# Two transformer layers with memory attention on one core: first segment in two token halves, loads tied to attention units, one pool of tiles, queries and keys projected two segments ahead

## The chip, the cores and the metric

The kernel runs on one core of a Trainium2 chip. A core has a matrix engine (TensorE, PE in the profile), a vector engine (VectorE, DVE), a scalar engine (ScalarE, ACT), a general engine (GpSimd, POOL) and an engine that issues transfers (SyncE, SP); ACT and POOL issue transfers too. Each engine has its own list of instructions, written in a fixed order, and waits on semaphores where the program says so. The matrix engine writes to PSUM, which the kernel takes as one tensor of 128 x 4096 f32, cut into eight banks of 512 columns; everything else is kept in SBUF. The metric is device time in microseconds.

## The reference

Two layers, each an attention block A and a feed-forward block B with the same weights, over 2048 tokens of width 512. Attention has 32 heads of width 16 and goes over the tokens in four segments of 512: causal attention inside a segment, and a memory of all earlier segments.

```python
q, k, v = heads(x @ wq), heads(x @ wk), heads(x @ wv)      # [B, H, N=4, L=512, 16]
phi = lambda t: jnp.where(t > 0, t + 1.0, jnp.exp(t))
g = sigmoid(beta)
for s in range(N):
    logits = einsum('bhqd,bhkd->bhqk', qs, ks) * scale + mask
    a_dot = einsum('bhqk,bhkd->bhqd', softmax(logits), vs)
    num = einsum('bhld,bhde->bhle', phi(qs), M)
    den = einsum('bhld,bhd->bhl', phi(qs), z)[..., None] + 1e-06
    outs.append(g * num / den + (1.0 - g) * a_dot)
    M = M + einsum('bhld,bhle->bhde', phi(ks), vs)
    z = z + einsum('bhld->bhd', phi(ks))
A = concat(outs) @ wo
B = (silu(x @ w1) * (x @ w3)) @ w2                          # width 1376 between
# x = x + A(layernorm(x)); x = x + B(layernorm(x)); both once more
```

## The kernel before

**A planner writes the order.** build() does not emit instructions. It adds operations to a list, each with the engines that may run it, an estimated duration, what it reads and writes, the tiles (bufs) that it holds, and a priority (lower goes first). schedule() then plays the list through once before anything is emitted: it lets each engine take, among the operations whose inputs would be there soon, the one of lowest priority, and so fixes one list for each engine. Tiles come from pools (ring()): an operation that needs a new tile is taken when one is free. finalize() derives the semaphore waits from the true dependences alone. Two things only steer the planner: a gate says that an operation may not be planned before another one has been, and a hold reserves a tile early. A gate leaves no wait in the program: on the chip, an operation with a gate starts as soon as its engine comes to it.

**The work of one segment.** A global segment g = 4 * layer + s has these stages:

- layer_norm (xa): statistics (bn_stats, bn_aggr) on VectorE, a power on POOL, the normalised tile xn on VectorE, and for each of four tiles of 128 tokens a transposing transfer xa<-xn issued by SP.
- project: twelve jobs of four matmuls each with 512 columns, in the order q0 k0 q1 k1 v0 v1 v2 v3 q2 k2 q3 k3 (the number is a group of eight heads for q and k, a token tile for v). Each job fills one PSUM bank of pool B (four banks); ACT or VectorE, whichever the planner picks, evicts it. km is a copy of k in which the even heads are zero: for g of 0 and 1 by VectorE, later by four transfers.
- phi: features of q and k: exp on ACT (px), two operations on VectorE (pq, pk).
- memory_read, for s > 0: 16 small matmuls give the denominators, VectorE takes reciprocals (rm), then four groups of matmuls give numerators, each in its own bank of pool B, each taken off by one VectorE operation (om).
- attention: 20 units. Each unit is a group of matmuls for logits (R in the planner, 16 and 32 rows of the array each) into pool S, one exp on ACT over 128 x 2048 elements, masks on POOL where a block touches the diagonal; every few units a group of matmuls with v (C) follows, an eviction xs, a transposing transfer xg<-xs, a normalisation og and a transposing transfer ot<-og. The list HALVES holds segment 0: it is done in two token halves, six units and fourteen, and, through SPLIT, with two exps of 1024 for each unit.
- memory_update: transposes of pk (pkt<-pk), matmuls with v, an addition to macc, a masked copy mb.
- out_proj: 16 matmuls with wo, added to x_tok on VectorE.
- layer_norm (xf) and ffn: 88 matmuls for gate and up, tanh on ACT, two VectorE operations each, and 44 matmuls down, added to x_tok. The priorities of ffn are the weakest; its matmuls fill PE while attention waits for ACT, and what is left is done at the end.

**What decides when projections come.** In project, job n of segment g is gated to attention unit (3n)//2 of segment g - 1 (line 547 and after). The layer_norm of g is gated to unit 10 of g - 2.

**Tiles of 4 KB per partition.** They lie in separate rings: xa 2, xf 1, q 2, k 2, pq 1, pk 1, pkt 1, ot 1, and km 2.

**Loads.** At the start SP issues x0, x2, wq, wv; ACT issues x1, x3, wk, x4 to x7, beta. late_loads gives the rest to POOL: wo, x8 to x11, x12 to x15, w1, w3 and w2 in halves and a remainder. Its gates name attention units of segment 0, so the planner puts the loads between POOL's masks, but no wait follows from them. wo comes out first on POOL.

**Constants.** clear_slot zeroes a va tile and writes ones for the denominators: slot 0 on VectorE, slot 1 on POOL by later_constants, which also clears km slot 1 and macc on POOL.

Of the kernel before, what the change touches and what calls it, by code (L numbers as in the profile page):

```python
# [59 lines left out]
class Sched:  # L60
# [15 lines left out]
    def add(self, opts, fn, reads=(), writes=(), bufs=(), prio=0.0, mode=None, dmaq=None, name="", gates=(), size=0,  # L76
            hold=()):
# [17 lines left out]
        for w in writes:  # L95
            p = self.res_w.get(w)
            if p is not None:
                deps[p.seq] = p
            for rd in self.res_r.get(w, ()):
                if rd is not op:  # L100
                    deps[rd.seq] = rd
            self.res_w[w] = op
            self.res_r[w] = []
        op.deps = deps
# [246 lines left out]
def build(nc, A_x, A_wq, A_wk, A_wv, A_wo, A_beta, B_w1, B_w3, B_w2, out):  # L351
# [26 lines left out]
    xa_r = ring("xa", 2, [P, NCG, 512])  # L378
    xf_r = ring("xf", 1, [P, NCG, 512])
    q_r = ring("q", 2, [P, NCG, 512])  # L380
    k_r = ring("k", 2, [P, NCG, 512])
    km_r = ring("km", 2, [P, NCG, 512])
    pq_r = ring("pq", 1, [P, NCG, 512])
    pk_r = ring("pk", 1, [P, NCG, 512])
    px_r = ring("px", 2, [P, 2, 512])
    pkt_r = ring("pkt", 1, [P, NCG, LT, P])
# [6 lines left out]
    ot_r = ring("ot", 1, [P, NCG, 512])  # L393
# [66 lines left out]
    def clear_slot(i, eng, gates):  # L460
        z = eng(lambda e: e.memset(va_r[i][:], 0.0), 3104, writes=[("va0", i)], prio=-50.0, gates=gates)
        o = eng(lambda e: e.memset(vheads(va_r[i], slice(0, LT), 0, H)[:, :, :, 16:17], 1.0), 128, writes=[("va0", i)], prio=-50.0,
                gates=gates)
        pools["va"].prev[i] = [z, o]

    clear_slot(0, dve, [])

    def later_constants(gates):
        clear_slot(1, pool, gates)
        pools["km"].prev[1] = [pool(lambda e: e.memset(km_r[1][:], 0.0), 2048, writes=[("km0", 1)], prio=0.5, gates=gates)]  # L470
        pool(lambda e: e.memset(macc[:], 0.0), 544, writes=[("macc", 0), ("macc", 1)], prio=1.0, gates=gates)
# [3 lines left out]
    for i in range(4):  # L475
        dma(("sp", "act")[i % 2], x_tok[:, i, :], xv[:, i, :], 131072, prio=CP - 10 + i, writes=[("x", i)], name="ldx%d" % i)

    def ldw(q, t, src, key, prio, gates=(), reads=()):
        dma(q, t[:], src.rearrange("(g p) f -> p g f", p=P), 524288, prio=prio, writes=[key], reads=reads, name="ld" + key)
    ldw("sp", wq_sb, A_wq, "wq", CP + 1)  # L480
    ldw("act", wk_sb, A_wk, "wk", CP + 2)
    ldw("sp", wv_sb, A_wv, "wv", CP + 3)
# [3 lines left out]
    def late_loads(after):  # L486
        for i in range(2, 4):
            dma("pool", x_tok[:, 4 * i:4 * i + 4, :], xv[:, 4 * i:4 * i + 4, :], 524288, prio=CP + i, gates=[units[(0, 8 * i - 9)]],
                writes=[("x", 4 * i + j) for j in range(4)], name="ldx")
        ldw("pool", wo_sb, A_wo, "wo", CP + 1.5, gates=[units[(0, 3)]])  # L490
        for a in range(2):
            for n, (t, src, key) in enumerate(((w1_sb, B_w1, "w1"), (w3_sb, B_w3, "w3"))):
                dma("pool", t[:, 2 * a:2 * a + 2, :], src[256 * a:256 * a + 256, :].rearrange("(g p) f -> p g f", p=P), 704512,
                    prio=CP + 4, gates=[units[(0, 5 + 4 * a + 2 * n)]], writes=[key + str(a)], name="ld" + key)
        for a in range(2):
            dma("pool", w2_sb[:, 5 * a:5 * a + 5, :], B_w2[640 * a:640 * a + 640, :].rearrange("(t p) d -> p t d", p=P), 655360,
                prio=CP + 6, gates=[units[(0, 13 + 2 * a)]], writes=["w2%d" % a], name="ldw2")
        dma("pool", w2_sb[0:96, 10, :], B_w2[1280:1376, :], 98304, prio=CP + 7, gates=[units[(0, 17)]], writes=["w22"], name="ldw2")
# [9 lines left out]
    def layer_norm(s, name, prio, gates=(), fine=False, part=(0, LT), dst=None):  # L508
        st = new("ln")
        dst = dst or new(name)  # L510
        tiles = range(*part)
        dt_ = {"xa": xa_r, "xf": xf_r}[name]
# [23 lines left out]

    class Seg:
        pass

    def project(s, g, X, first):  # L540
        z = Seg()
        z.q, z.k, z.km, z.va = new("q"), new("k"), new("km"), new("va")
        jobs = [("q", 0), ("k", 0), ("q", 1), ("k", 1), ("v", 0), ("v", 1), ("v", 2), ("v", 3),
                ("q", 2), ("k", 2), ("q", 3), ("k", 3)]
        if first:
            jobs = [("q", 0), ("k", 0), ("q", 1), ("k", 1), ("v", 0), ("v", 1), ("q", 2), ("k", 2), ("q", 3), ("k", 3),
                    ("v", 2), ("v", 3)]
        for n, (kind, G) in enumerate(jobs):
            p0 = g - 0.95 + 0.05 * n
            gate = units.get((g - 1, (3 * n) // 2))  # L550
            B = new("B")
            for cg in range(NCG):
                st, sp_ = cg == 0, cg == NCG - 1
                if kind == "v":
                    fn = lambda e, cg=cg, G=G, B=B, st=st, sp_=sp_: e.matmul(  # L555
                        bank(B), xa_r[X.slot][:, cg, 128 * G:128 * G + 128], wv_sb[:, cg, :], start=st, stop=sp_)
                    rd = [(X, G)]
                else:
                    w = wq_sb if kind == "q" else wk_sb
                    fn = lambda e, cg=cg, G=G, B=B, st=st, sp_=sp_, w=w: e.matmul(  # L560
                        bank(B), w[:, cg, 128 * G:128 * G + 128], xa_r[X.slot][:, cg, :], start=st, stop=sp_)
                    rd = [(X, i) for i in range(LT)]
                pe(fn, MM512, reads=rd + ["w" + kind], writes=[(B, 0)], bufs=[B, X], prio=p0 + 0.001 * cg - 500, gates=[gate],
                   hold=[{"q": z.q, "k": z.k, "v": z.va}[kind]],
                   name="%s%d.%d" % (kind, G, cg))
            if kind == "v":
                ev(lambda G=G: vheads(va_r[z.va.slot], G, 0, H)[:, :, 0:16], lambda B=B: bank(B).rearrange("p (h d) -> p h d", d=DH), 512,
                   reads=[(B, 0)], writes=[(z.va, G)], bufs=[B, z.va], prio=p0 - 100, name="evv")
            else:
                t, b = (q_r, z.q) if kind == "q" else (k_r, z.k)  # L570
                ev(lambda G=G, t=t, b=b: t[b.slot][:, G, :], lambda B=B: bank(B), 512, reads=[(B, 0)], writes=[(b, G)],
                   bufs=[B, b], prio=p0 - 100, name="ev" + kind)
                if kind == "k" and g <= 1:
                    dve(lambda e, G=G: e.tensor_scalar(km_r[z.km.slot][:, G, :], k_r[z.k.slot][:, G, :], cm[1][:, 0:1], None,
                                                       op0=ALU.mult), 512, mode=1.5,
                        reads=[(z.k, G), "cm1"], writes=[(z.km, G)], bufs=[z.k, z.km], prio=p0 + 0.02, name="km")
                elif kind == "k" and G == NCG - 1:
                    for pg in range(4):
                        r = slice(32 * pg + 16, 32 * pg + 32)
                        S.add([("sp", 450.0, 2200.0)], lambda e, r=r: e.dma_start(km_r[z.km.slot][r], k_r[z.k.slot][r]), dmaq="sp",  # L580
                              mode="T", reads=[(z.k, a) for a in range(NCG)], writes=[(z.km, pg, "p")], bufs=[z.k, z.km],
# [386 lines left out]
```

## Time and profile before

| | |
|---|---|
| median of 8 runs | 563.83 us (562.42 to 566.53) |
| the profiled execution's own time | 563.86 us |
| its span in the profile | 562.1 us |
| mean granted TensorE clock | 0.945 |
| instructions | 10266 |
| moved by DMA | 36.89 MB |
| read from HBM | 8.43 MB |

The page cuts the span into 40 slices of 14.05 us and shows one digit for each: the busy share of an engine in tenths, or the clock that TensorE was granted in tenths of full speed. A window line gives, for a stretch of time, its length, then for PE, PEld (weight loads, which lie beside matmuls), DVE, ACT and POOL the busy time and the count, then the granted clock, the busy share of the DMA engines and GB/s. A timeline line gives start, duration, engine, line, operation, output and inputs, count, and in brackets how long the engine had been idle and what ended that. SPq and ACTq lines are issues of transfers.

### The profile page before, as it was taken

What the parts mean: (1) busy time and instruction counts of PE and PEld (TensorE: products, weight loads), DVE (VectorE), ACT (ScalarE), POOL (GpSimd) and SP (SyncE); (2) the same over time, 40 slices, a digit from 0 to 9 for tenths busy, and PEclk for the clock granted to TensorE, in tenths of its full rate; (3) what the DMA queues carried; (4) which work ended last, traced back from release to release, by engine and by line L of the source; (5) the groups of instructions that cost most, each with busy time, mean ns of one, the idle gap of its engine ahead of it and who ended that gap; (6) DMA issues with size and microseconds to landing.
All of it is one profiled execution on the core that took longest, in us unless ns stands there. A gap on an engine that the chain in (4) does not pass through costs nothing.

```text
span 562.1 us, 10266 instructions
## 1 busy us (share of the span) xinstructions
PE 495.8 (88%) x4050; PEld 211.4 (38%) x4120; DVE 409.7 (73%) x807; ACT 399.0 (71%) x352; POOL 234.2 (42%) x345
## 2 busy tenths in 40 slices
PE   0975796988998999998889999889997999999997
PEld 0321243345444333333333333333343333444443
DVE  7386659788878888868676977976679656767573
ACT  0696787799989888888896888869895888213130
POOL 6184424355455655555342554325642445100000
PEclk9975798899999999999996999979999999999999
DMA  9166945233211422331332223322232032020301
GB/s 241 21 175 149 183 86 83 45 79 75 31 35 39 94 48 48 62 82 39 56 57 48 49 47 67 73 34 55 58 58 39 22 83 56 20 76 0 76 0 37
DMA packets 107584, 36.89 MB, mean 66 GB/s; under 512 B 101297, under 2 KB 105905, under 8 KB 107537
## 3 DMA queue, kind: packets, MB, share of 16 engines
q1 hardware_dynamic: 104640, 29.12, 26.6%
q0 software_dynamic: 1408, 5.80, 3.3%
q10 hardware_dynamic: 1488, 1.32, 0.7%
q8 instruction: 32, 0.52, 0.4%
q14 instruction: 16, 0.12, 0.1%
HBM read 8.43 MB, written 2.10 MB: 19 GB/s over the span
## 4 chain that ended last, share of the span: by engine, by line
PE 57%; DVE 19%; DMA 10%; ACT 9%; issue 3%; POOL 1%; SPq 0%; POOLq 0%
PE psall L863 21%; PE psall L891 11%; PE psall L560 7%; ACT e L730 7%; PE psall L722 6%; PE psall L767 4%; PE psall L832 4%; DMA xg<-xs 3%; DVE ln L515 3%; DMA xa<-xn 3%; PE psall L555 3%; DMA pkt<-pk 2%; DVE x_tok L836 1%; DVE gp L876 1%; ACT px L590 1%
## 5 line engine op out<-in xcount | busy, mean ns | idle before, releaser
L730 ACT ACTIVATE e<-psall 128x2048 bf16<-128x2048 f32 (+1 forms) x180 | 300.9, 1691 | 58.9 <-PE psall L722 56.7
L743 POOL TENSOR_SCALAR_AFFINE_SELECT e<-e 128x512 bf16<-128x512 bf16 x256 | 163.0, 656 | 215.1 <-ACT e L730 214.6
L863 PE MATMUL psall<-xf,w 128*128 128x512 bf16 (+3 forms) x770 | 172.8, 360 | 5.5 <-DVE om L660 2.0
L863 PEld LDWEIGHTS psall<-xf,w 128*128 128x128 bf16 (+1 forms) x792 | 74.6, 101 | 85.1 <-issue 13.7
L874 ACT ACTIVATE th<-psall 128x512 bf16<-128x512 f32 (+2 forms) x89 | 51.7, 593 | 61.8 <-PE psall L863 61.6
L891 PE MATMUL psall<-w,h 128*128 128x512 bf16 (+1 forms) x336 | 83.5, 380 | 1.2 <-issue 0.8
L876 DVE SCALAR_TENSOR_TENSOR gp<-th,psall 128x512 bf16<-128x512 bf16 (+2 forms) x89 | 59.3, 675 | 23.2 <-ACT th L874 22.8
L880 DVE SCALAR_TENSOR_TENSOR h<-gp,psall 128x512 bf16<-128x512 bf16 (+1 forms) x89 | 59.7, 673 | 18.2 <-PE psall L863 18.0
L767 PE MATMUL psall<-e,va 128*32 128x256 bf16 (+3 forms) x1088 | 51.5, 318 | 4.2 <-POOL e L743 1.5
L555 PE MATMUL psall<-wv,xa 128*128 128x512 bf16 x121 | 36.3, 399 | 20.1 <-DMA xa<-xn 19.3
L722 PE MATMUL psall<-q,k 16*128 16x256 bf16 (+3 forms) x544 | 44.0, 308 | 10.6 <-ACT e L730 8.4
L722 PE MATMUL psall<-q,km 32*128 32x256 bf16 (+3 forms) x544 | 44.1, 308 | 3.0 <-ACT e L730 2.6
L891 PEld LDWEIGHTS psall<-w,h 128*128 128x128 bf16 (+1 forms) x352 | 31.8, 97 | 38.9 <-issue 7.1
L896 DVE TENSOR_TENSOR x_tok<-psall,x_tok 128x512 bf16<-128x512 f32 x32 | 22.0, 688 | 30.9 <-PE psall L891 30.8
L515 DVE BATCH_NORM_STATS2 ln<-x_tok 128x6 f32<-128x512 bf16 x64 | 42.9, 680 | 0.9 <-DMA x_tok<-in_A_x_dram 0.2
L832 PE MATMUL psall<-wo,ot 128*128 128x512 bf16 x121 | 32.9, 400 | 7.4 <-DMA ot<-og 6.0
L767 PEld LDWEIGHTS psall<-e,va 128*32 128x32 bf16 x1088 | 24.4, 102 | 39.8 <-POOL e L743 16.5
L528 DVE TENSOR_SCALAR xn<-x_tok,ln 128x512 bf16<-128x512 bf16 x64 | 34.2, 560 | 5.9 <-DMA xa<-xn 2.8
L560 PE MATMUL psall<-xa,wk 128*128 128x512 bf16 x119 | 33.6, 389 | 2.7 <-issue 0.8
L560 PE MATMUL psall<-xa,wq 128*128 128x512 bf16 x119 | 33.8, 389 | 1.8 <-DVE gp L876 0.7
L722 PEld LDWEIGHTS psall<-q,k 16*128 16x128 bf16 x544 | 13.3, 93 | 54.1 <-ACT e L730 39.8
L446 DVE CAST xs<-psall 128x512 bf16<-128x512 f32 x37 | 25.2, 681 | 6.8 <-PE psall L767 6.7
(66 smaller groups left out, 431.7 us busy)
## 6 DMA issues: line engine op xcount, KB each, us to landing
w<-in_B_w_dram POOLq DMA_DIRECT2D x4, 688.0 KB, 5.6
out_dram<-x_tok SPq DMA_DIRECT2D x16, 128.0 KB, 1.8
km<-k SPq DMA_DIRECT2D x24, 64.0 KB, 2.4
w<-in_B_w_dram POOLq DMA_DIRECT2D x2, 640.0 KB, 6.5
xg<-xs SPq DMA_TRANSPOSE x64, 2.4
x_tok<-in_A_x_dram POOLq DMA_DIRECT2D x2, 512.0 KB, 5.4
ot<-og SPq DMA_TRANSPOSE x36, 2.4
wo<-in_A_wo_dram POOLq DMA_DIRECT2D x1, 512.0 KB, 8.9
```

The costliest lines, as they stand in the source:

```text
L515: dve(lambda e, i=i, tt=tt: e.bn_stats(ln_r[st.slot][:, i, 0:6], x_tok[:, tt, :]), 540, reads=[("x", tt)], writes=[(st, 0, i)], bufs=[st], ...
L555: fn = lambda e, cg=cg, G=G, B=B, st=st, sp_=sp_: e.matmul(bank(B), xa_r[X.slot][:, cg, 128 * G:128 * G + 128], wv_sb[:, cg, :], start=st, ...
L560: fn = lambda e, cg=cg, G=G, B=B, st=st, sp_=sp_, w=w: e.matmul(bank(B), w[:, cg, 128 * G:128 * G + 128], xa_r[X.slot][:, cg, :], start=st ...
L722: o = e.matmul(S4[:, sps(pg), c:c + n], kk[32 * pg:32 * pg + r, G, 128 * j:128 * j + 128], q_r[z.q.slot][32 * pg:32 * pg + r, G, 128 * t1 ...
L730: act(lambda e, N=N, ebuf=ebuf, pgs=pgs, sps=sps: e.activation(e_r[ebuf.slot][:, pgs[0]:pgs[-1] + 1, 0:N], S4[:, sps(pgs[0]):sps(pgs[-1]) ...
L743: pool(lambda e, ebuf=ebuf, c=c: e.affine_select(e_r[ebuf.slot][:, :, c:c + 128], e_r[ebuf.slot][:, :, c:c + 128], pattern=[[0, 4], [1, 128]],
L767: o = e.matmul(bank(X)[32 * pg:32 * pg + 32, base + W - n:base + W], va_r[z.va.slot][:, j, h:h + 32], e_r[eb.slot][:, pg, c:c + n], start= ...
L832: pe(lambda e, i=i, G=G, B=B: e.matmul(bank(B), ot_r[z.ot.slot][:, G, 128 * i:128 * i + 128], wo_sb[:, G, :], start=(G == 0), stop=(G == N ...
L863: prev = pe(lambda e, i=i, cg=cg, ft=ft, B=B, w=w: e.matmul(bank(B)[0:width(ft), W * i:W * i + W], w[:, cg, 128 * ft:128 * ft + width(ft)] ...
L876: dve(lambda e, fw=fw, NW=NW, B=B, th=th, gp=gp: e.scalar_tensor_tensor(gp_r[gp.slot][0:fw, 0:NW], th_r[th.slot][0:fw, 0:NW], 1.0, bank(B) ...
L880: dve(lambda e, fw=fw, NW=NW, B=B, gp=gps[fg], h=hs[fg]: e.scalar_tensor_tensor(h_r[h.slot][0:fw, 0:NW], gp_r[gp.slot][0:fw, 0:NW], 0.5, b ...
L891: prev = pe(lambda e, ft=ft, fw=fw, B=B, h=h, c=c: e.matmul(bank(B), h_r[h.slot][0:fw, c:c + 128], w2_sb[0:fw, ft, :], start=(ft == 0), st ...
```

## The change

- Segment 0 is projected in two token halves: q and k jobs take two head groups with 256 columns each (eight matmuls in one bank) in place of one group with 512. The order is q01 k01 v0 v1 q23 k23 for tokens 0 to 255, then q01 k01 v2 v3 q23 k23 for the others. Dependences of q, k and km are kept by half, so that the logits of the first half need only the first.
- The first loads are put in order of use: SP x0, wq, x2; ACT x1, wk, x3, wv, x4 to x7, beta.
- The loads on POOL get a true wait (after=) on PE's logits of the unit that gates them, in a new order: x8 to x11 after unit 1, wo after 3, w1 and w3 after 5 to 11, w2 after 13 to 17, x12 to x15 after 18.
- The second va tile and macc are cleared on VectorE after unit 2; km is no longer cleared.
- xa, xf, q, k, pq, pk, pkt and ot come from one pool W of 11 tiles.
- For g of 2 and more, q and k jobs are gated to units 12 to 19 of segment g - 2 and v jobs to units 0 to 6 of g - 1 (release); all q and k come before v. The four km transfers get a priority and a gate of their own.
- WARM is 0, so the block under it adds nothing.

```diff
@@ add
-            hold=()):
+            hold=(), after=()):
...
+        for d in after:
+            deps[d.seq] = d
@@ build
-    xa_r = ring("xa", 2, [P, NCG, 512])
-    xf_r = ring("xf", 1, [P, NCG, 512])
-    q_r = ring("q", 2, [P, NCG, 512])
-    k_r = ring("k", 2, [P, NCG, 512])
+    w_r = ring("W", 11, [P, NCG, 512])
+    xa_r = xf_r = q_r = k_r = pq_r = pk_r = ot_r = w_r
     km_r = ring("km", 2, [P, NCG, 512])
-    pq_r = ring("pq", 1, [P, NCG, 512])
-    pk_r = ring("pk", 1, [P, NCG, 512])
-    pkt_r = ring("pkt", 1, [P, NCG, LT, P])
+    pkt_r = [t[:].rearrange("p g (i c) -> p g i c", i=LT) for t in w_r]
-    ot_r = ring("ot", 1, [P, NCG, 512])
...
     def later_constants(gates):
-        clear_slot(1, pool, gates)
-        pools["km"].prev[1] = [pool(lambda e: e.memset(km_r[1][:], 0.0), 2048, writes=[("km0", 1)], prio=0.5, gates=gates)]
-        pool(lambda e: e.memset(macc[:], 0.0), 544, writes=[("macc", 0), ("macc", 1)], prio=1.0, gates=gates)
+        clear_slot(1, gates)
+        dve(lambda e: e.memset(macc[:], 0.0), 544, writes=[("macc", 0), ("macc", 1)], prio=1.0, gates=gates)
...
-    for i in range(4):
-        dma(("sp", "act")[i % 2], x_tok[:, i, :], xv[:, i, :], 131072, prio=CP - 10 + i, writes=[("x", i)], name="ldx%d" % i)
+    ldx("sp", 0, CP - 10)
+    ldx("act", 1, CP - 9)
     ldw("sp", wq_sb, A_wq, "wq", CP + 1)
     ldw("act", wk_sb, A_wk, "wk", CP + 2)
-    ldw("sp", wv_sb, A_wv, "wv", CP + 3)
+    ldx("sp", 2, CP + 2.1)
+    ldx("act", 3, CP + 2.2)
+    ldw("act", wv_sb, A_wv, "wv", CP + 3)
...
+    def late(out_ap, in_ap, size, n, keys, name):
+        dma("pool", out_ap, in_ap, size, prio=CP + n, gates=[units[(0, n)]], after=[units[(0, n)]], writes=keys, name=name)
...
+    def release(g, n):
+        if g < 2:
+            return units.get((g - 1, 2 + (3 * n) // 2))
+        return units.get((g - 2, 12 + n)) if n < 8 else units.get((g - 1, 2 * (n - 8)))
@@ project
-        jobs = [("q", 0), ("k", 0), ("q", 1), ("k", 1), ("v", 0), ("v", 1), ("v", 2), ("v", 3),
-                ("q", 2), ("k", 2), ("q", 3), ("k", 3)]
         if first:
-            jobs = [("q", 0), ("k", 0), ("q", 1), ("k", 1), ("v", 0), ("v", 1), ("q", 2), ("k", 2), ("q", 3), ("k", 3),
-                    ("v", 2), ("v", 3)]
+            jobs = []
+            for hf in range(2):
+                for A in (0, 2):
+                    jobs += [("q", (A, A + 1), hf), ("k", (A, A + 1), hf)]
+                jobs[4 * hf + 2 * hf + 2:4 * hf + 2 * hf + 2] = [("v", (2 * hf,), 0), ("v", (2 * hf + 1,), 0)]
+        else:
+            jobs = [(k, (G,), None) for G in range(NCG) for k in ("q", "k")] + [("v", (i,), 0) for i in range(LT)]
...
-            gate = units.get((g - 1, (3 * n) // 2))
+            gate = release(g, n)
...
+                        fn = lambda e, cg=cg, G=G, B=B, st=st, sp_=sp_, w=w, a=a, W=W, c0=c0: e.matmul(
+                            bank(B)[:, W * a:W * a + W], w[:, cg, 128 * G:128 * G + 128], xa_r[X.slot][:, cg, c0:c0 + W],
+                            start=st, stop=sp_)
+                        rd = [(X, i) for i in range(c0 // 128, c1 // 128)]
```

## The prediction

> **What bounds the kernel now.** I read the page first (busy shares and slices), then the windows of 20 and 5 us, then the timeline of the first 80 us, then the waits, then the order in which each engine gets its instructions in the two kernels.
>
> ```profile
> PE 495.8 (88%) x4050; PEld 211.4 (38%) x4120; DVE 409.7 (73%) x807; ACT 399.0 (71%) x352; POOL 234.2 (42%) x345
> PE   0975796988998999998889999889997999999997
> PEclk9975798899999999999996999979999999999999
> ```
>
> TensorE (PE) has the most work, and it is full only after the first fifth. The three places to see are the empty first slice, the hole in slices 3 to 7 with the clock at half, and three later slices with the clock digit at 6, 9 and 7. The windows put numbers to them (columns: window, busy PE, PEld, DVE, ACT, POOL with counts, clock, DMA share, GB/s):
>
> ```profile
> 0.00:20.00 20.00, 4.96 (x17) 2.02 (x18) 11.65 (x23) 3.06 (x5) 9.71 (x16) 1.00 0.74 184
> 40.00:60.00 20.00, 13.52 (x137) 5.08 (x140) 13.23 (x38) 13.73 (x15) 9.83 (x14) 0.50 0.78 185
> 480.00:500.00 20.00, 19.89 (x92) 9.29 (x93) 16.02 (x34) 2.98 (x5) 3.38 (x4) 1.00 0.23 53
> 50.00:55.00 5.00, 1.87 (x6) 0.61 (x9) 3.48 (x9) 0.50 (x1) 3.50 (x4) 0.50 0.29 64
> 430.00:435.00 5.00, 2.87 (x53) 1.64 (x54) 4.97 (x13) 3.70 (x3) 2.84 (x4) 0.93 0.05 11
> ```
>
> From 480 us on PE is 99% busy at full clock: a fixed tail of dense matmuls. So a microsecond taken from any stall before it is a microsecond at the end, provided that the same work has been issued by then. Counting (window minus busy times clock) over all 20 us windows gives 88 us of lost PE time, 51 of them before 120 us. The start and segment 0, in the timeline:
>
> ```profile
> 7.08 7.12 DVE L528 TENSOR_SCALAR xn<-x_tok,ln 128x512 bf16<-128x512 bf16 x4 [0.41 <-POOL ln L522]
> 7.52 7.90 SPq L532 DMA_TRANSPOSE xa<-xn  x4
> 8.56 2.67 POOL L461 MEMSET va<- 128x3104 bf16 x1
> 15.04 2.72 PE L555 MATMUL psall<-wv,xa 128*128 128x512 bf16 x6 [15.04 <-DMA xa<-xn]
> 23.44 14.00 ACT L730 ACTIVATE e<-psall 128x1024 bf16<-128x1024 f32 x15 [0.17 <-PE psall L722]
> 53.13 1.91 PE L832 MATMUL psall<-wo,ot 128*128 128x512 bf16 x4 [4.62 <-DMA ot<-og]
> 55.62 1.02 ACT L730 ACTIVATE e<-psall 128x1024 bf16<-128x1024 f32 x1 [5.12 <-PE psall L722]
> ```
>
> The first matmul waits 15.04 us for a transpose; the first exp follows 8.40 us later. Then ScalarE (ACT) sets the pace: 15 exps in 14.00 us, 0.93 each. At 53 us PE, which takes its instructions in order, stands 4.62 us before an output projection whose transpose is late, and ACT runs dry for 5.12 us behind it. The 40th and last exp of segment 0 ends at 75.04.
>
> **What the Trainium skill says.** "DMA: Bandwidth & Descriptors", section "Queues, rings and completion order": each issuing queue has its own ring on every DMA engine, served in ring order, and the engine goes round-robin between rings. The trace agrees: the first transpose, issued at 7.52 on SP's ring behind wq and wv, takes up to 7.4 us to land where the usual one takes 2.4. "SBUF — State Buffer", "SBUF: two separate sides": VectorE and GpSimd share one port pair as an exclusive lock. It agrees: of the four xn instructions three take 0.41 us and the fourth 5.56, exactly while the POOL memsets run (8.56 to 14.05). "TensorE: Matmul & The Clock Gate", Part 1: an idle window of some 3.4 us halves the clock. It agrees: 35 to 60 us is granted 0.50, and 365 to 370 after idle time 0.60.
>
> **The change, part by part.**
>
> *Start.* wo (512 KB, issued by POOL at 1.38 us) leaves the first burst and is held for attention unit 3. x0 and x1 go first, then wq on SP and wk on ACT, then x2, x3; wv moves to ACT's ring. VectorE now does two statistics instead of four before the first xn: 2 x 0.66 = 1.3 us earlier, so xn0 at 5.8, transposes issued at about 6.2 and 7.5 (1.26 apart in the trace). They stand behind x0, wq and x2 on SP, 0.79 MB, while ACT's ring moves as much. The trace moved 0.8 MB in the first 5 us and 333 GB/s after: 1.57 MB by 7.3 us. So the transposes land between 9.9 (7.5 + 2.4, free) and 14.9 (7.5 + 7.4, as crowded as now); I take 10.5. First matmul: 15.04 to 10.5, 4.5 us.
>
> *Two halves.* First matmul to first exp is now six v, then four jobs of four matmuls (8.40 us). Afterwards it is 16 matmuls of 256 columns, cold, half of the 0.425 us spacing seen for 512: 3.4 us; the eviction 0.60 and km 0.35; while PE does seven v matmuls (about 2.0 at mixed clock, these end last). With the handovers 5.7 us. Saves 2.7. The 32 additional weight loads (0.10 each, 3.2 us) run beside PE; if uncovered, they cost up to 3.2 in a stage where ACT has the say; I take 0. First exp: 23.4 to 16.2. Bounds of this part: 2.7 to 7.8 us; I take 7.2. The second half's x2, x3 land near 9, their xn near 12.5, transposes near 15: in time for a second half projected after 20 us, so no cost.
>
> *Memsets.* POOL loses 2.67 + 1.79 + 0.67 + 0.87 us, whose removal is what frees the fourth xn. VectorE gains one va memset (1.35 + 0.17) and macc (by its share of 1552 words, 0.5): 2.0 us, after unit 2, in a window where it is 13.85 of 20 busy. Hidden by exps; if not, one xs eviction is late by 1.4 us.
>
> *True waits.* POOL waits for PE's logits of unit n before it issues a load; behind it stand only masks of units that come later, so 0. The loads, now in nine steps of at most 0.70 MB per two units (3.7 us of exps), ask for 190 GB/s at most; before, four issues between 36.05 and 43.22 put 2.6 MB into some ten microseconds (293 GB/s from 40 to 45 us), and xg and ot transposes took 4.5 and 3.8 us instead of 2.4. Segment 0 has 40 exps (37.6), two px (2.0) and two xs (1.2) on ACT, 40.8 us, out of 51.6; 10.8 are idle. In the new order one px comes after the last exp, but two evictions and gth join: 41.0. The distance from the last probability product of the first half to the output projection is still seven exps, so that wait isn't designed away; only faster transposes shorten it. Idle after: 2 at best, 10.8 at worst; I take 6. Saves 4.8. Milestone "last exp of segment 0": 75.0 to 16.2 + 41.0 + 6 = 63.2, 12 us earlier.
>
> *One pool, two segments ahead.* The old rings held 2+1+2+2+1+1+1+1 = 11 tiles, the pool has 11: no more storage, only free use of it. From the orders, I summed columns at 2.4 per ns up to the end of each segment's logits (row- and column-tiled matmuls by four): 22.3 us before and 22.5 after at segment 0, 235.9 and 239.1 at segment 5, 330.3 and 331.0 at segment 7, out of 413.7 in both. So the milestone gain isn't borrowed from work left for the tail. The sums of Q and K alone show the lead is at most 3.4 us of columns (half a segment), and in most half-segments there is none. What it can mend are the transitions: at 295, 367 and 432 us VectorE is at 4.47 to 4.97 of 5 us with query features, reciprocal, four om of 0.62 us and residual additions in a heap, PE waits and then runs cold; those three cost 6.1, 6.6 and 4.9 us in their windows of 20, 17.6 together. In the new VectorE order the reciprocal and the four om stand ahead of the residuals also for the last segment, but still in one run. I take a quarter mended: 4 us. Bounds: 17 gained, or (below) 20 lost.
>
> Sum against the profiled run's 563.86 (span 562.1, 1.8 around it): 563.9 - 7.2 - 4.8 - 4 = 547.9. The median shown, 563.83, is the same. Forecast 548.
>
> **The rivals.** *Small gain, 557:* the transposes are as late as now in the first 15 us (2.7 instead of 7.2) and the output projection stalls as before; 4 from the transitions. For it: the DMA share is 1.30 from 10 to 15 us, and the same seven exps of distance. Against: wo is gone and SP carries less ahead of the transposes.
>
> *Large gain, 535:* idle in segment 0 falls to 2 and the three cold transitions go: 563.9 - 7.2 - 8.8 - 13 = 534.9. Against: the om instructions remain in one run.
>
> *Slower, 568:* the four numerator groups of a memory read take all four PSUM banks of pool B and hold PE until VectorE's reciprocal and om free them. Three such events cost 17.6 now and the one near 95 us some 6. If the new order makes all six memory reads (segments 1 to 3 and 5 to 7) stall by the dearest of these, 6.6, the steady part loses 39.6 - 23.6 = 16: 563.9 - 12 + 16 = 567.9. It decides once the transitions lose more than the milestone's 12. For it: four om in one run in most segments, and VectorE at 4.97 of 5 us there already. Against: both orders have nearly the same density, and the features of Q are evicted and computed no later than now.
>
> *It doesn't run ahead:* Q and K of segment 2 first appear in PE's order after segment 1's fifth unit, hardly earlier than now. Then that part is worth 0: 552, inside the forecast's range.
>
> **How the numbers follow.** Forecast with "doesn't run ahead" (540 to 555) 0.55, small gain (555 to 562) 0.15, large gain (under 540) 0.14, slower 0.13, nothing 0.03. A change under 0.3% (1.7 us) can't be told from none. Faster 0.84, same 0.03, slower 0.13. The range, a tenth left out at each side: 536 to 564; the likeliest case alone, 540 to 555.
>
> **What would show it.** First matmul at 9.9 to 11, first exp near 16, last exp of segment 0 near 63; no POOL memset beside an xn; transposes from 30 to 60 us near 2.5 to 3.5 us; tail of about 83 us at full clock as now. Wrong if the first matmul is still near 14, if the wait at the output projection is over 4 us, or if the clock row has more than three dips after 100 us.

## The result

The changed kernel takes 556.73 us (median of 11 runs, 553.37 to 560.64), against 563.8 for the kernel before (32 runs): ratio 0.9869, 95% interval [0.9845, 0.9893]. It is 7.1 us or 1.3% faster, where 15.8 us or 2.8% was forecast. Its profiled execution took 554.05 us, its span is 552.3, 9.8 shorter than before (562.1).

The lines of the page (busy times, and 40 slices, now of 13.8 us), after:

```profile
PE 491.1 (89%) x4086; PEld 213.9 (39%) x4152; DVE 411.5 (75%) x821; ACT 394.6 (71%) x344; POOL 227.8 (41%) x338
PE   1973797979999989999979999799997999999997
PEclk9985798999999999999989999899998999999999
```

Slices 3 to 5 still show the clock at 8, 5, 7 (it was 7, 5, 7). The cold spots in the steady part are shallower: 8, 8, 8 where 6, 9, 7 stood. The windows (columns as before):

```profile
0.00:20.00 20.00, 8.23 (x59) 4.56 (x59) 8.30 (x24) 5.37 (x7) 3.62 (x12) 1.00 0.56 158
40.00:60.00 20.00, 10.37 (x115) 4.11 (x109) 13.42 (x36) 10.42 (x12) 8.23 (x11) 0.57 0.59 153
480.00:500.00 20.00, 19.89 (x92) 9.07 (x93) 14.28 (x30) 2.98 (x5) 1.01 (x1) 1.00 0.21 53
45.00:50.00 5.00, 0.00 (x0) 0.10 (x1) 4.93 (x16) 0.00 (x0) 1.86 (x3) 0.50 0.16 44
```

PE has 3.3 us more behind it at 20 us, and 3.2 us less work done between 40 and 60. From 45 to 50 us it did nothing at all, and neither did ACT. The same instructions in the timeline as were shown of before:

```profile
6.02 0.94 DVE L542 TENSOR_SCALAR xn<-x_tok,ln 128x512 bf16<-128x512 bf16 x2 [0.54 <-POOL ln L536]
6.46 6.38 SPq L546 DMA_TRANSPOSE W<-xn  x4
11.76 1.89 PE L586 MATMUL psall<-W,wq 128*128 128x256 bf16 x8 [11.76 <-DMA W<-xn]
17.70 5.61 ACT L762 ACTIVATE e<-psall 128x1024 bf16<-128x1024 f32 x6 [0.39 <-PE psall L753]
49.86 0.10 PEld L864 LDWEIGHTS psall<-wo,W 128*128 128x128 bf16 x1 [8.27 <-DMA W<-og]
50.40 0.29 PE L753 MATMUL psall<-W 16*128 16x128 bf16 x2 [8.33 <-DMA W<-og]
50.94 1.03 PE L864 MATMUL psall<-wo,W 128*128 128x512 bf16 x2
51.05 1.02 ACT L762 ACTIVATE e<-psall 128x1024 bf16<-128x1024 f32 x1 [7.01 <-PE psall L753]
```

The start is 5.7 us earlier at the first exp (17.70 for 23.44). At the output projection of the first half PE now stands 8.33 us, where it stood 4.62, and ACT is dry for 7.01 us instead of 5.12. (The first matmuls of the projection are not recorded in this trace; its weight load, PEld L864, shows the wait, and the 8.33 reach on to the next recorded matmul.) Cut at the last exp of each segment, the profiled executions compare as follows (us; of the last columns, the sum of segments 1 to 7 and what follows the last exp):

| | seg 0 | 1 | 2 | 3 | 4 | 5 | 6 | 7 | 1 to 7 | tail |
|---|---|---|---|---|---|---|---|---|---|---|
| before | 75.0 | 60.9 | 51.5 | 53.7 | 58.5 | 55.1 | 59.2 | 62.2 | 401.1 | 85.9 |
| after | 72.1 | 60.8 | 51.8 | 55.0 | 55.5 | 55.7 | 54.6 | 61.3 | 394.7 | 85.5 |

So of 9.8 us 2.9 come from segment 0, 6.4 from segments 1 to 7, 0.4 from the tail. From the first exp to the 40th takes 54.4 us; before it was 51.6. The early start was half lost again in segment 0.

### The profile page after: what moved, and what is told of

Its sections match the earlier page's. It is cut to its first block, busy times and chain, and to the rows that moved or that the text cites. A ratio compares the mean times of both kernels' runs of the same rounds, so it can differ in the third digit from the quotient of the medians.

```text
span 552.3 us, 10350 instructions
## 1 busy us (share of the span) xinstructions
PE 491.1 (89%) x4086; PEld 213.9 (39%) x4152; DVE 411.5 (75%) x821; ACT 394.6 (71%) x344; POOL 227.8 (41%) x338
## 4 chain that ended last, share of the span: by engine, by line
PE 61%; DVE 15%; DMA 13%; ACT 5%; issue 3%; POOL 2%; SPq 0%; ACTq 0%; POOLq 0%; DVEq 0%
PE psall L895 21%; PE psall L923 12%; PE psall L586 7%; PE psall L753 6%; PE psall L799 5%; PE psall L864 4%; DMA W<-xn 4%; DMA xg<-xs 4%; ACT e L762 4%; DMA W<-og 3%; PE psall L581 2%; PE psall L645 2%; DVE ln L529 2%; DVE gp L908 1%; DMA W<-W 1%
## 5 line engine op out<-in xcount | busy, mean ns | idle before, releaser
L762 ACT ACTIVATE e<-psall 128x2048 bf16<-128x2048 f32 (+1 forms) x180 | 300.9, 1696 | 62.6 <-PE psall L753 60.9
L895 PE MATMUL psall<-W,w 128*128 128x512 bf16 (+2 forms) x768 | 173.3, 358 | 7.5 <-issue 2.5
L895 PEld LDWEIGHTS psall<-W,w 128*128 128x128 bf16 (+1 forms) x792 | 73.0, 100 | 83.7 <-issue 16.0
L906 ACT ACTIVATE th<-psall 128x512 bf16<-128x512 f32 (+2 forms) x89 | 52.0, 592 | 58.1 <-PE psall L895 57.9
L753 PE MATMUL psall<-W 16*128 16x256 bf16 (+3 forms) x544 | 42.5, 305 | 16.3 <-DMA W<-og 8.3
L586 PE MATMUL psall<-W,wq 128*128 128x512 bf16 (+1 forms) x138 | 36.0, 371 | 13.6 <-DMA W<-xn 12.3
L753 PE MATMUL psall<-W,km 32*128 32x256 bf16 (+3 forms) x544 | 42.1, 301 | 2.0 <-ACT e L762 1.7
L581 PE MATMUL psall<-wv,W 128*128 128x512 bf16 x121 | 33.9, 393 | 5.0 <-DMA W<-xn 4.1
L586 PE MATMUL psall<-W,wk 128*128 128x512 bf16 (+1 forms) x138 | 35.4, 366 | 0.5 <-issue 0.5
L443 DVE CAST W<-psall 128x512 bf16<-128x512 f32 x41 | 27.8, 684 | 10.6 <-PE psall L586 9.3
L864 PE MATMUL psall<-wo,W 128*128 128x512 bf16 x120 | 32.9, 404 | 2.6 <-DMA W<-og 1.9
L753 PEld LDWEIGHTS psall<-W 16*128 16x128 bf16 x544 | 13.1, 93 | 49.6 <-ACT e L762 38.5
```

Source lines behind the costliest of these rows:

```text
L443: return e.tensor_copy(dst(), src())
L586: fn = lambda e, cg=cg, G=G, B=B, st=st, sp_=sp_, w=w, a=a, W=W, c0=c0: e.matmul(bank(B)[:, W * a:W * a + W], w[:, cg, 128 * G:128 * G + 1 ...
L753: o = e.matmul(S4[:, sps(pg), c:c + n], kk[32 * pg:32 * pg + r, G, 128 * j:128 * j + 128], q_r[z.q.slot][32 * pg:32 * pg + r, G, 128 * t1 ...
L762: act(lambda e, N=N, ebuf=ebuf, pgs=pgs, sps=sps: e.activation(e_r[ebuf.slot][:, pgs[0]:pgs[-1] + 1, 0:N], S4[:, sps(pgs[0]):sps(pgs[-1]) ...
L864: pe(lambda e, i=i, G=G, B=B: e.matmul(bank(B), ot_r[z.ot.slot][:, G, 128 * i:128 * i + 128], wo_sb[:, G, :], start=(G == 0), stop=(G == N ...
L895: prev = pe(lambda e, i=i, cg=cg, ft=ft, B=B, w=w: e.matmul(bank(B)[0:width(ft), W * i:W * i + W], w[:, cg, 128 * ft:128 * ft + width(ft)] ...
```

## The experiments

The first reading (theory A) was that the new load order puts w1 and w3 exactly on the first half's transposes. Rivals: the seven exps of distance to the projection are too short whatever the transposes take; or the true waits do the harm. The steady part had its own question: is it the lead of two segments, or merely another list from the planner?

**Later output projection** (changed kernel, one gate added):

```diff
-                   prio=g + 0.9 + 0.001 * i - 900, name="o%d" % i)
+                   prio=g + 0.9 + 0.001 * i - 900, name="o%d" % i, gates=[units.get((0, 15))] if g == 0 and i < 2 else ())
```

> The changed kernel with one more gate for the planner: the output projection of segment 0's first half comes in PE's order after unit 15, 13 exps behind the half's last probability product where it was 7. Nothing is added or left out. Theory A (transfers of the first half's transposes are slowed by the weight loads to 5 to 9 us, and PE stands in order before the projection): the wait for W<-og before the projection falls from 8.3 us to under 2, the transposes themselves stay at 5 to 9 us, the 40th exp ends near 65 to 66 instead of 72.1, ratio to the kernel before about 0.975. Rival B (segment 0 is bound by the transfers as a whole, wherever PE waits): the wait moves to the next transposed input, the 40th exp stays at 70 to 72, ratio 0.985 to 0.99. Rival C (a gain here is given back in the segments after it): 40th exp near 66, ratio still 0.985 to 0.99.

Measured: 558.91 us, ratio 0.9912 [0.988, 0.9944]. With thirteen exps of distance the wait is gone, and the 40th exp ends at 65.2. But segments 1 to 7 take 410.8, segment 7 alone 72.8. That part, in the windows of this run and then in its timeline:

```profile
425.00:430.00 5.00, 2.26 (x18) 0.54 (x16) 3.63 (x6) 2.53 (x2) 1.22 (x2) 0.50 0.53 107
430.00:435.00 5.00, 5.00 (x32) 1.45 (x32) 1.28 (x2) 2.36 (x2) 0.64 (x1) 0.50 0.13 29
```

```profile
423.42 1.06 DVE L542 TENSOR_SCALAR xn<-x_tok,ln 128x512 bf16<-128x512 bf16 x3 [0.32 <-POOL ln L536]
424.39 0.28 DVE L673 TENSOR_SCALAR rm<-psall 128x128 f32<-128x128 f32 x1
424.91 0.95 DVE L675 RECIPROCAL rm<-rm 128x128 f32<-128x128 f32 x1
426.22 2.48 DVE L691 TENSOR_TENSOR om<-psall,rm 128x512 bf16<-128x512 f32 x4
```

In this list residual additions and the normalisation of other tokens stand on VectorE from 416 to 425 us ahead of the memory read's chain (rm, om); PE runs dry, then goes on at half clock. q and k of segment 7 come late in this list: their last eviction ends 18.6 us after the last exp of segment 6, where it is 8.8 in the changed kernel. One gate in segment 0 has changed the order in segment 7: the planner's list is new everywhere.

**Later loads** (w1, w3, w2 in units 13 to 19 instead of 5 to 17, x12 to x15 after 19):

```diff
-                     5 + 4 * a + 2 * n, [key + str(a)], "ld" + key)
+                     13 + 2 * a + n, [key + str(a)], "ld" + key)
...
```

> The changed kernel with w1, w3 and w2 held for units 13 to 19 instead of 5 to 17. Nothing is added or left out. Theory A: with only x and wo in the way the first half's transposes land in 2.3 to 3 us, the wait before its output projection falls from 8.3 us to under 1, the 40th exp ends near 65; the second half's and segment 1's transposes are slowed instead, so that 2 to 4 us come back: ratio 0.98. Rival B (not the weight loads, but the planned distance): transposes still 5 to 9 us, wait 6 to 8 us, ratio 0.987. Rival D (the loads come too late for the feed-forward part): PE waits for w1 or w2 after 80 us, ratio 0.99 or more.

Measured: 555.65 us, 0.9886 [0.9843, 0.9929]. No wait at the projection, 40th exp at 63.6, 8.5 us earlier than in the changed kernel; transposes issued from 25 to 50 us land in 2.4 us (median). Segments 1 to 7 take 400.7, 6.0 more. In time that is no gain: 1.1 us between the medians, and the profiled execution (551.62 us) is the fastest of its six. But in this list the projection also stands ten exps behind the first half's last product with v, instead of seven, so this run alone doesn't separate slow transposes from short distance.

**Small loads.** This separates them: the planner is told the old sizes, so every instruction stays in its place, but only 128 columns of each half of w1 and w3 and one of five row blocks of each half of w2 are loaded, and used for all. Most feed-forward weights are left out.

```diff
-                late(t[:, 2 * a:2 * a + 2, :], src[256 * a:256 * a + 256, :].rearrange("(g p) f -> p g f", p=P), 704512,
+                late(t[:, 2 * a:2 * a + 2, 0:128], src[256 * a:256 * a + 256, 0:128].rearrange("(g p) f -> p g f", p=P), 704512,
...
-            late(w2_sb[:, 5 * a:5 * a + 5, :], B_w2[640 * a:640 * a + 640, :].rearrange("(t p) d -> p t d", p=P), 655360,
+            late(w2_sb[:, 5 * a, :], B_w2[640 * a:640 * a + 128, :], 655360,
...
```

> The changed kernel with the order on every engine untouched, but w1 and w3 loaded for their first 128 columns alone and w2 for one of five row blocks; the matmuls read these columns in place of the others, so most of the feed-forward weights are left out and the load traffic of segment 0 falls from 5.8 to about 2.0 MB. Theory A: transposes of 30 to 46 us land in 2.3 to 3.5 us instead of 5 to 8.7, the wait before the first half's output projection falls from 8.3 us to under 1, the 40th exp ends at 61 to 64 instead of 72.1. If a microsecond of segment 0 is a microsecond at the end, as the prediction took it, segments 1 to 7 keep their 395 us and the whole is 545 to 547, ratio 0.967 to 0.971. Rival C (given back): segment 1 grows by 2 to 6 us, because PE has to do what it did in the stall or its transposes are late for another reason; ratio 0.975 to 0.982. Rival B: the wait stays over 5 us, ratio 0.987.

Measured: 549.71 us, 0.9767 [0.9729, 0.9805]. The DMA issues from 25 to 50 us (KB each, median us from issue to landing), first in the changed kernel, then in this one:

```profile
w<-in_B_w_dram POOLq DMA_DIRECT2D x4, 688.0 KB, 6.4
xg<-xs SPq DMA_TRANSPOSE x5, 5.0
W<-og SPq DMA_TRANSPOSE x4, 4.5
```

```profile
w<-in_B_w_dram POOLq DMA_DIRECT2D x4, 64.0 KB, 2.7
xg<-xs SPq DMA_TRANSPOSE x5, 3.0
W<-og SPq DMA_TRANSPOSE x4, 2.4
```

And in this run's timeline:

```profile
34.68 0.51 PE L799 MATMUL psall<-e,va 128*32 128x256 bf16 x16
...
35.98 3.39 DVE L623 TENSOR_SCALAR W<-W 128x1024 bf16<-128x1024 bf16 x2
39.30 0.68 DVE L529 BATCH_NORM_STATS2 ln<-x_tok 128x6 f32<-128x512 bf16 x1
39.90 0.67 DVE L443 CAST xs<-psall 128x512 bf16<-128x512 f32 x1
...
47.10 0.29 PE L753 MATMUL psall<-W 16*128 16x128 bf16 x2 [5.39 <-DMA W<-og]
47.74 1.02 ACT L762 ACTIVATE e<-psall 128x1024 bf16<-128x1024 f32 x1 [4.07 <-PE psall L753]
```

In the same order and with transposes back at 2.4 to 3.0 us, the projection starts 3.3 us earlier and the 40th exp ends at 65.3, 6.8 us earlier. The other 3.5 us arise after the projection, where the loads of w2 are small too: from 53 to 61 us the transposes land in 2.5 us (median) for 4.9. The clock from 50 to 70 us is 0.83 instead of 0.67; it is at 0.50 until 57 us in both runs, but falls to 0.50 again from 63.9 to 70.8 in the changed kernel alone. Segments 1 to 7 take 396.3, 1.6 more, so most of the gain arrives at the end: 5.2 us in the span, 7.0 in the medians.

So theory A holds for the loads as a whole: they cost segment 0 these 6.8 us. But a wait of under 1 us was expected at the projection, and 5.39 us remain with no heavy load beside it. So the rival is right in part: seven exps are too few for the chain of eviction, transpose, normalisation and second transpose. The trace shows where most of the chain's time goes. The first half's last product with v ends at 35.19, and its eviction xs begins only at 39.90, 4.7 us later, because VectorE has a normalisation, km, two features of k or q (L623) and a statistic before it. These two features take 3.39 us here, beside four masks on POOL, where they took 1.62 in the changed kernel. The two transposes that follow take 2.38 and 2.27. No run moved this eviction forward.

**No true waits** (`after=[units[(0, n)]]` taken from the loads on POOL, gates kept):

```diff
-        dma("pool", out_ap, in_ap, size, prio=CP + n, gates=[units[(0, n)]], after=[units[(0, n)]], writes=keys, name=name)
+        dma("pool", out_ap, in_ap, size, prio=CP + n, gates=[units[(0, n)]], writes=keys, name=name)
```

> The changed kernel without the true waits of the loads (gates for the planner only, new order kept). Theory A: POOL's masks already pace the loads, so they go out at most 2 us earlier, the first half's wait stays at 6 to 10 us, ratio 0.985 to 0.99. Rival E (the waits themselves hold POOL back and its masks with it): masks come earlier, ratio 0.98 or lower. Rival F (the waits are worth what the change claims for them): x8 to x11 go out in the first burst, first matmul later by 1 us or more, ratio 0.99 to 1.0.

Measured: 556.1 us, 0.9883 [0.986, 0.9907], the same as the changed kernel. The four w1 and w3 halves are issued at 28.66 to 39.08, for 29.01 to 40.16 with the waits. The wait at the projection is 4.0 us for 8.3, less than the 6 to 10 that were expected (the list is new here as well), the 40th exp 2.1 earlier at 70.0, and segments 1 to 7 take 398.3, 3.6 more. The waits did not spread the loads to any use; they are not what the gain rests on.

**One segment ahead** (old gates for projections of g from 2, with the old order of jobs; pool W kept):

```diff
-        return units.get((g - 2, 12 + n)) if n < 8 else units.get((g - 1, 2 * (n - 8)))
+        return units.get((g - 1, (3 * n) // 2))
...
```

> The changed kernel with the old gates of the projections (one segment ahead) and the old order of jobs (v in the middle) for segments 1 to 7; pool W, halves and loads as changed. My account of the steady part (the lead mended a part of the three cold transitions, about 4 us): the time from the 40th exp of segment 0 to the end goes from 480 back to 484 to 487 us, ratio 0.993 to 1.0. Rival G (the lead does nothing, the free pool of tiles does): 480 us stays, ratio 0.987. Rival H (the gain of the steady part is the planner's accident): anything between 475 and 495.

Measured: 560.49 us, 0.9929 [0.9905, 0.9953]; segments 1 to 7 take 400.7, as before the change. Taken alone this speaks for the lead: 6.0 us between the traces, 3.8 between the medians. The next runs show why it isn't enough.

**Another list.** LAT is the planner's estimate of a handover between engines. 60 became 65 and 55, in the changed kernel and in the one before; no operation, size or dependence changes, only the order that comes out, and the engine where the planner has a choice.

```diff
-LAT = 60.0
+LAT = 65.0
```

> The changed kernel with one number of the planner altered, the handover between engines that it assumes: 65 ns instead of 60. No work is added, moved by intent or left out. It measures what replanning alone does. If the steady part is governed by the lead of the projections, segments 1 to 7 stay within 3 us of 394.7 and the ratio within 0.983 to 0.991. If the planner's accident governs it (rival H), single segments differ by 4 us or more from those of the changed kernel (60.8, 51.8, 55.0, 55.5, 55.7, 54.6, 61.3), and the sum by 5 us or more.

> As the kernel with 65 ns, with 55 ns: the second sample of replanning alone. Lead: segments 1 to 7 together 392 to 398 us. Accident: further away than that.

> The kernel before with the planner's handover estimate LAT at 65 instead of 60; nothing else. Question: does the changed kernel's shorter steady part (segments 1 to 7 take 394.7 us in it, 402.9 and 397.1 with LAT 65 and 55, 401.1 in the kernel before) come from the common pool and the longer lead, or is it the spread that any other list of the planner gives? Theory 'pool and lead': the kernel before stays at 400 us or above for segments 1 to 7 with either LAT, ratio 0.997 to 1.02. Theory 'spread': one of the two values brings it to 395 to 398 us, ratio 0.99 to 0.995. In both its segment 0 ends near 75 us, since its transposes, loads and first burst are the same.

> The kernel before with LAT at 55. As for LAT 65: 'pool and lead' expects segments 1 to 7 at 400 us or above and a ratio of 0.997 to 1.02, 'spread' one of the two at 395 to 398 us and a ratio of 0.99 to 0.995. The mean over the three lists (60, 65, 55) against the changed kernel's mean of 398.2 us is the test: 3 us or more apart speaks for the pool, under 2 us for spread.

| LAT | before: us | segs 1 to 7 | after: us | segs 1 to 7 |
|---|---|---|---|---|
| 60 | 563.8 | 401.1 | 556.73 | 394.7 |
| 65 | 564.85 | 402.0 | 560.95 | 402.9 |
| 55 | 562.76 | 400.4 | 555.38 | 397.1 |

Ratios: changed kernel with 65 and 55, 0.9966 [0.9945, 0.9987] and 0.9882 [0.9841, 0.9922]; kernel before, 1.0035 [1.0008, 1.0062] and 1.0008 [0.9987, 1.003]. The mean steady part is 401.2 before and 398.2 after: 3.0 us, just at the mark that was set beforehand as speaking for the pool, but with a spread of 8 us over three lists of the changed kernel against 1.6 before. So the sum alone does not show that the change shortens the steady part, nor that the 6.0 us between the run with one segment ahead and the changed kernel are the lead's. The whole change, over three lists each, is worth 6.1 us in the means of the medians.

The segments taken singly tell more. Call q and k of a segment late by the time from the last exp of the segment before to the end of their last eviction:

| segment 6 | q and k late by, us | time, us |
|---|---|---|
| before, LAT 60, 65, 55 | 6.2, 5.5, 6.9 | 59.2, 57.4, 57.9 |
| after, LAT 60, 65, 55 | -5.7, -5.6, -4.4 | 54.6, 55.1, 56.0 |
| one segment ahead | 8.1 | 62.0 |
| start alone | 13.4 | 68.3 |

Between the two means that is 2.9 us, nearly all of the 3.0. In all fourteen traces segment 6 takes 54.2 to 56.0 us where q and k are more than 4 us early (seven of them), and 57.4 or more where they are not. Segments 2 to 5 had q and k 6 to 9 us early before the change, and have them 20 to 44 us early in the three lists after it; together they take 219.0 us before and 219.6 after. Segment 7 is late in every trace. So a lead that makes late inputs early goes with a gain of about 3 us, and a longer one with none. This is a reading of the traces: the lists differ in other things too, and no run moved q and k of segment 6 alone.

**Start alone** (kernel before with its rings and projections; new load order at the start, wo with a true wait after unit 3, va slot 1 and macc cleared on VectorE):

```diff
-        clear_slot(1, pool, gates)
-        pools["km"].prev[1] = [pool(lambda e: e.memset(km_r[1][:], 0.0), 2048, writes=[("km0", 1)], prio=0.5, gates=gates)]
+        clear_slot(1, dve, gates)
...
+    ldx("sp", 0, CP - 10)
+    ldx("act", 1, CP - 9)
...
-        ldw("pool", wo_sb, A_wo, "wo", CP + 1.5, gates=[units[(0, 3)]])
+        ldw("pool", wo_sb, A_wo, "wo", CP + 1.5, gates=[units[(0, 3)]], after=[units[(0, 3)]])
```

> The kernel before with only the new start: first loads in order of use, wo held by a true wait on unit 3, the second va tile and macc cleared on VectorE after unit 2, km not cleared. No halves, old rings, projections one segment ahead. My account: first matmul near 12.5 (it needs only one tile for v, but q waits for all four, so PE stops between), first exp near 21 instead of 23.4, 40th exp 2 to 3 us earlier than 75.0, ratio about 0.995. Rival (the halves alone make the early start, the loads do nothing): first exp at 23 to 24, ratio 1.0. Rival (the fourth xn, freed of the memsets, is what counts): first exp at 18 to 19, ratio 0.99.

Measured: 566.88 us, 1.0074 [1.0041, 1.0108]: slower, although the first exp is at 20.9 (2.6 earlier) and the 40th ends at 70.4 (4.6 earlier). Segments 6 and 7 take 68.3 and 74.5; q and k are late there by 13.4 and 20.5 us (the tail is 6.2 shorter). So load order and memsets are worth 2.6 us at the first exp, the two halves the other 3.2. At the first matmul they are worth everything: it comes at 11.42 here and at 11.76 in the changed kernel, and what the halves shorten is the way from there to the first exp, from 9.4 us here to 5.9. And a gain in the start can be lost again, and more, in a list that happens to be poor.

**Two candidates.** Later loads with the output projection after unit 12, and later loads with LAT 55:

> A candidate to beat both: the changed kernel with the feed-forward weights loaded in units 13 to 19 and the first half's output projection planned after unit 12. If the two causes of the stall in segment 0 add, there is no wait before that projection, the 40th exp ends at 63 to 65 us and, with segments 1 to 7 at 396 to 401 us, the time is 547 to 553 us, ratio 0.971 to 0.981. If the planner's new list gives it back (as it did with the later projection alone), segments 1 to 7 take 405 us or more and the time is 556 us or more.

> A second candidate: loads in units 13 to 19 as above, the output projection where the planner puts it, LAT at 55. Segment 0 as with the later loads alone (40th exp near 64 us); if the list of LAT 55 is as good here as with the early loads (segments 1 to 7 at 397 us), the time is 548 to 551 us, ratio 0.973 to 0.978; if the list is worse (401 us or more), 553 us or more, no better than the changed kernel.

Measured: 556.59 us, 0.9881 [0.9846, 0.9915], and 555.65 us, 0.9862 [0.9825, 0.9898]. Neither beats the changed kernel beyond the intervals. In the first the long wait is gone, but ten short waits of ACT before its exps add to 9.2 us in segment 0, PE has a clock of 0.59 from 50 to 70 us, and the 40th exp ends at 70.9; the two causes do not add. The second reaches 65.0 and loses it in segment 1 (69.1), in a profiled execution that is the slowest of its five (559.31 us):

```profile
59.48 0.89 POOL L433 DMA_DIRECT2D w<-in_B_w_dram  x1 [0.26 <-PE psall L753]
61.21 0.87 POOL L433 DMA_DIRECT2D w<-in_B_w_dram  x1 [0.18 <-issue]
...
70.75 1.08 PE L645 MATMUL psall<-va,W 128*128 128x136 bf16 x8 [7.78 <-DMA W<-W]
```

The loads that no longer meet xg and og now stand beside the transposes of pk (the one issued at 57.83 lands after 12.87 us), and PE waits 7.78 us before memory_update (L645). The collision was moved, not removed.

## Why the prediction was wrong

The sign and the places were right, the size was not. By the steps of its sum, on the profiled executions:

| step | forecast | measured |
|---|---|---|
| start, to the first exp | -7.2 | -5.7 |
| first to 40th exp | -4.8 (and 0.2 of new work) | +2.8 |
| segments 1 to 7 (transitions) | -4 | -6.4 |
| tail | 0 | -0.4 |
| sum | -16.0 | -9.8 |

The medians differ by 7.1, since the profiled execution of the changed kernel lies 2.7 us under its median.

- **Failed: true waits (the idle of 6 us).** The step put ACT's work from the first to the 40th exp at 41.0 us and its idle time at 6, between 2 and 10.8. The work is 41.0; the idle time, 10.8 before, is 13.4, outside these bounds (12.9 and 13.3 with the two other lists). The prediction held that loads spread over nine steps would bring the transposes of 30 to 60 us "near 2.5 to 3.5 us". From 25 to 50 us xg and og transposes land in 5.0 and 4.5 us; in the kernel before it was:

```profile
xg<-xs SPq DMA_TRANSPOSE x4, 4.7
ot<-og SPq DMA_TRANSPOSE x3, 5.1
```

  So there was no relief. Single ones got worse: an og transpose issued at 32.64 took 8.7 us, one at 36.15 (xg) 7.6. I averaged the demand (190 GB/s) over a stretch in which a transpose meets a load or doesn't. Starting 6 us earlier, the four w1 and w3 halves (issued at 29.01 to 40.16) fell on the first half's chain. With small loads in the same order the idle time is 7.2 us, near the 6 that the step assumed. So this is the term that was mis-sized, by 7.6 us: -4.8 turned into +2.8. The prediction's own criterion for being wrong, over 4 us at the output projection, was met: 8.3. Its rival of a stalled projection came nearest in time (557), but for a different sum: the start was better and the stall worse than it said.
- **Start: right in kind, 1.5 us short.** The xn pair is at 6.02 for 5.8, transposes issued at 6.46; no memset stands beside an xn and all four take 0.41. The second transpose, issued at 7.81, landed after 3.9 us where the forecast left it 3.0, while the loads issued before it were still landing (the last at 10.86). First matmul 11.76 for 10.5, inside the bounds of 9.9 to 14.9; first matmul to first exp 5.94 for 5.7. The run with the start alone gives the earlier first matmul to the load order and the memsets, and the shorter way to the first exp to the halves.
- **Distance of seven exps: right.** It was named as not designed away. With small loads and quick transposes PE still waits 5.4 us there; the late eviction on VectorE, which the prediction had no term for, is part of it.
- **Transitions: size near, cause shown in part.** The three cold windows of 20 us lost 17.6 us of PE and the dearest three windows after 280 us now lose 13.5 (3.5 from 280, 5.0 from 340, 5.0 from 400): 4.1 less, as forecast. But they did not disappear, they moved. At the start of segment 7, in the timeline of the changed kernel:

```profile
416.89 0.95 DVE L675 RECIPROCAL rm<-rm 128x128 f32<-128x128 f32 x1
418.20 2.48 DVE L691 TENSOR_TENSOR om<-psall,rm 128x512 bf16<-128x512 f32 x4
419.82 0.40 PE L753 MATMUL psall<-W 16*128 16x256 bf16 x4 [2.46 <-DMA km<-W]
420.49 1.88 ACT L762 ACTIVATE e<-psall 128x2048 bf16<-128x2048 f32 x1 [4.55 <-PE psall L753]
```

  q and k of segment 7 are projected from 404 to 414 us, at the end of segment 6 and later, not two segments ahead: their tokens come out of the feed-forward of global segment 3, whose weak priority delays it. The four om stand in one run, as the prediction said they still would, and the km transfers come late (issued at 414.23 to 417.40, the last landed at 419.78). "It doesn't run ahead" is what happens here, in segment 7. No other segment has its q and k two segments ahead either: the longest lead is one segment, for segment 3 (132 to 141 us, its first exp at 186). What goes with the gain is segment 6, whose q and k came late before and come early now.
- **"A microsecond taken from any stall before it is a microsecond at the end": right only with a fixed order.** With small loads, where the order is kept, 5.2 of 6.8 us arrive. Where the planner makes a new list, 8.5 (later loads) or 6.9 (later projection) arrive as 2.4 us in the span or as a loss of 5.8 (in the medians, a gain of 1.1 and a loss of 2.2). The prediction gave the list's luck no term; over LAT alone the changed kernel's time differs by 5.6 us, 1.0%.
- **The clock: misread.** The prediction saw its two dips (from 35 us, and 365 to 370 us) agree with an idle window of some 3.4 us. No such window stands before them. The last 3.4 us before each fall, in windows of the kernel before:

```profile
31.50:34.90 3.40, 1.76 (x38) 0.79 (x37) 3.27 (x8) 3.40 (x5) 3.39 (x7) 1.00 0.58 98
362.60:366.00 3.40, 1.75 (x19) 0.56 (x15) 3.40 (x9) 0.66 (x2) 1.90 (x2) 1.00 0.58 101
```

  PE was busy half of the time, with no gap over 0.6 us in the first case and 1.03 in the second; the long wait, from 48.51 us, came later. In the changed kernel too the clock falls at 36.6 us, after 3.4 us with 1.75 of PE, and before the wait that begins at 42.1. So the stall of the projection did not make that drop. What decides it is not shown.
- **Costed at nothing, and right:** 32 more weight loads (PEld 213.9 for 211.4 us, beside PE), the memsets of 1.35, 0.17 and 0.51 us on VectorE beside exps.

## What to carry to other kernels

Place a large load against the chains of small transposes by time, not by mean bandwidth: list what is issued in each of its microseconds, and what stands in order behind a late one. Where a planner rewrites the whole list, a single before-and-after pair says little about a mechanism: keep the order fixed (small transfers under the planned sizes) to price a wait, and run a few equivalent lists to see the spread that any other change must exceed. A gain at one place has to be followed to the last segment before it is counted. And where work is moved ahead, compare for each segment when its inputs were there and when they were wanted, before and after: here a gain stood only where inputs had been late.

## What the runs showed of the hardware

A transposing transfer that lands in 2.3 to 2.4 us alone took up to 8.7 us beside weight loads that POOL had issued, and 12.87 us in the last candidate, with up to five loads under way. With loads of 64 instead of 688 KB the medians fell from 5.0 and 4.5 to 3.0 and 2.4. Not expected was the same small VectorE multiplication at ten times its usual time, both times beside four masks on POOL (timeline of the changed kernel, 0.17 us being usual):

```profile
29.77 2.39 POOL L775 TENSOR_SCALAR_AFFINE_SELECT e<-e 128x512 bf16<-128x512 bf16 x4
29.91 1.70 DVE L834 TENSOR_TENSOR rd<-rd,gg 128x16 f32<-128x16 f32 x1
...
44.06 0.17 DVE L834 TENSOR_TENSOR rd<-rd,gg 128x16 f32<-128x16 f32 x1
...
53.70 1.90 DVE L834 TENSOR_TENSOR rd<-rd,gg 128x16 f32<-128x16 f32 x1
53.76 2.39 POOL L775 TENSOR_SCALAR_AFFINE_SELECT e<-e 128x512 bf16<-128x512 bf16 x4
```

Of the 36 instructions of this line, the 19 that overlap no mask took 0.16 to 0.19 us; the 11 that overlap masks for 0.27 us or more took 0.22 to 1.90, about as long as the overlap. That fits the shared port of the Trainium skill ("SBUF — State Buffer", "SBUF: two separate sides"), where a VectorE operation with two SBUF inputs can be shut out by a GpSimd operation that reads SBUF; the prediction read the xn of the kernel before by the same section. The page speaks of one instruction; here the wait went on through three masks of 0.6 us in a row. No run took the masks away, so the cause is argued, not shown.
